# Attention with mixed heads: loads one per double step, half of them issued by GpSimd

## The chip, the cores and the metric

The kernel runs on one core of a Trainium2 chip. The metric is the time of one execution on the device in microseconds (us), lower is better; for the kernel before, three executions without a profile and one with it are shown.

## What is computed

Per batch (4 of them, 12 heads, 448 positions, 64 per head), scores of all heads are mixed by a 12 x 12 matrix before the softmax and by another one after it. The result goes through a token mixer and a channel mixer:

```python
scores = scale * np.matmul(q, k.transpose(0, 1, 3, 2))
scores = np.einsum('bhij,hg->bgij', scores, w_pre)
attn = softmax(scores)                      # over the last axis
attn = np.einsum('bhij,hg->bgij', attn, w_post)
x = np.matmul(attn, v)                      # then heads are joined: [4, 448, 768]
u = x + (np.maximum(x^T @ w_tok1, 0) @ w_tok2)^T
out = u + np.maximum(u @ w_ch1, 0) @ w_ch2
```

## The kernel before, in words

**Tiles.** A batch has four row tiles of 120, 120, 120 and 88 rows, so there are 16 tiles T. For a tile, `qk` (L140) computes the scores of a pair of heads in six calls and copies them to an SBUF tile `s`, on ScalarE (L156) or VectorE (L154). To mix heads on TensorE, the heads of ten rows have to lie along the partitions: `regroup` (L162, L164) moves them by a DMA from `s` into one of eight tiles `r`. There are 180 such groups.

**Steps.** Two groups make a step. `pre` (L166, L172) mixes the heads, `mx` (L180) takes the maximum on VectorE, `ex` (L189) the exponential on ScalarE, `rec` (L194) the reciprocal of the sums on VectorE and the product e with it on GpSimd (L203). `post` (L205, L214) mixes the heads again, `turn` (L229) transposes in blocks on VectorE, and `av` (L233, L246) multiplies by v for a pair of head pairs, ends in a copy on ScalarE (L253) and the sum x on GpSimd (L255), and leaves a store of x that `store` (L262) issues on SP later.

**Double steps.** The loop over J (L521) writes the program out, two steps at a time, and each engine runs its instructions in that order. Double step J holds the post of steps 2J and 2J+1, the softmax of the next two, the mixing of the two after those, the score groups that the table `score[J]` asks for and the value groups of `value[J]`. At its end come the four regroupings for steps 2J+8 and 2J+9 (L601) and the loads of `loads[J + 1]` (L604). A regrouping writes into an r that the mixing of the same double step has just read.

**Loads.** `load_q`, `load_k` and `load_v` (L104 to L135) fetch q of a tile, k of a batch in three pieces of two head pairs, and v of a batch in four parts. A load of q or k is two DMAs, one for partitions 0 to 63 and one for 64 to 127; the table `one` (L268) has SP issue both. Parts 2 and 3 of v are three DMAs each, which swap the halves of the partitions. Regroupings, loads and stores of x are all issued by SP and wait there in order. L505 to L514 fill the table of loads.

**Beginning and end.** Before the loop the first q and k are issued by SP and ScalarE, then q of tile 1 and part 0 of v by SP (L284, L285); the six score groups of tile 0 and the first eight regroupings follow (L310 to L313), and four score groups of tile 1 (L486). The last double steps and the stages after the loop (from L607) convert weights and run the two mixers; from about 330 us on they are long runs of matmuls.

Of the kernel before, what the change touches and what calls it, by code (L numbers as in the profile page):

```python
# [19 lines left out]
B, H, S, D = 4, 12, 448, 64  # L20
DM = H * D
DT, DC = 256, 1536
JT = 4
IT = [(0, 120), (120, 120), (240, 120), (360, 88)]
GR = 10
HP = H // 2
# [10 lines left out]
def attn_mixer_kernel(  # L37
# [12 lines left out]
    nc = tc.nc  # L50
# [34 lines left out]
    AT, V = {}, {}  # L85
# [15 lines left out]
    NT = len(first)  # L101
    first.append(NG)

    def load_k(b, h, m, eng):  # L104
        if b not in K:
            K[b] = early.tile([128, HP, S], F32, tag="k", bufs=2, name="k")
        for s in range(2):
            o = HP * s + h
            eng[s].dma_start(out=K[b][64 * s:64 * s + 64, h:h + m, :], in_=k[b, :, o:o + m, :])

    def load_q(T, h, m, eng):
        b, t = divmod(T, 4)
        i0, n = IT[t]
        if T not in Q:
            Q[T] = early.tile([128, HP, 120], F32, tag="q", bufs=3, name="q")
            if n < QP[t]:
                nc.gpsimd.memset(Q[T][:, :, n:QP[t]], 0.0)
        for s in range(2):
            o = H * i0 + (HP * s + h) * n
            eng[s].dma_start(  # L120
                out=Q[T][64 * s:64 * s + 64, h:h + m, :n],
                in_=q[b, :, o:o + m * n].rearrange("p (h i) -> p h i", h=m),
            )

    def load_v(b, part):
        if b not in V:
            V[b] = late.tile([128, H, JT, D], F32, tag="v", bufs=2, name="v")
        hs = slice(3 * part, 3 * part + 3)
        if part < 2:
            nc.sync.dma_start(out=V[b][:, hs], in_=v[b, :, hs])  # L130
            return
        lower, upper = slice(0, 64), slice(64, 128)
        nc.sync.dma_start(out=V[b][upper, hs, :3], in_=v[b, lower, hs, :3])
        nc.sync.dma_start(out=V[b][lower, hs, :3], in_=v[b, upper, hs, :3])
        nc.sync.dma_start(out=V[b][upper, hs, 3], in_=v[b, upper, hs, 3])  # L135

    def pair(tag, name):
        return (ps if tag == "pre" else ps_w).tile([128, 2, 512], F32, tag=tag, bufs=2, name=name)

    def qk(T, h, home="w", dve=False):  # L140
        b, t = divmod(T, 4)
        n = IT[t][1]
        if T not in S_t:
            S_t[T] = early.tile([120, H, S], F32, tag="s", name="s")
        p = pair(home, "qk")
        for c in (0, 64):
            m = min(64, QP[t] - c)
            for s in range(2):
                r = slice(64 * s, 64 * s + 64)
                nc.tensor.matmul(  # L150
                    out=p[c:c + m, s, :S], lhsT=Q[T][r, h, c:c + m], rhs=K[b][r, h, :], start=True, stop=True
                )
        if dve:
            nc.vector.tensor_copy(out=S_t[T][:n, h::HP, :], in_=p[:n, :, :S])  # L154
        else:
            nc.scalar.copy(out=S_t[T][:n, h::HP, :], in_=p[:n, :, :S])  # L156
# [109 lines left out]

    two = (nc.sync, nc.scalar)
    one = (nc.sync, nc.sync)  # L268
    load_q(0, 0, 2, two)
    load_k(0, 0, 1, two)  # L270
    load_k(0, 1, 2, two)
# [10 lines left out]
    for r in rt:  # L282
        nc.gpsimd.memset(r[:4], 0.0)
    load_q(1, 0, HP, one)  # L284
    load_v(0, 0)  # L285
    wz = et[0][:, 0].bitcast(BF16)
    nc.vector.memset(et[0], 0.0)
    for i in range(WARM):
# [4 lines left out]
    for x in range(2):  # L293
        ps_ = slice(64 * x, 64 * x + 64)
        nc.vector.tensor_tensor(
            out=kpre[ps_, :60].rearrange("p (i g) -> p i g", i=5),
# [5 lines left out]
    for s in range(2):  # L302
        ps_ = slice(64 * s, 64 * s + 64)
        for hf in range(2):
            nc.gpsimd.tensor_tensor(
                out=kpost[ps_, 32 * hf:32 * hf + 30].rearrange("p (g i) -> p g i", g=6),
# [165 lines left out]
    sf = [f // 2 for f in first]  # L472
    sl = [(f - 1) // 2 for f in first[1:]]
    loads = {J: [] for J in range(-2, ND)}
    score = {J: [] for J in range(-2, ND)}
    value = {J: [] for J in range(-2, ND)}
    for T in range(NT - 1):
        J = (sl[T] + 1) // 2
        n = sf[T + 2] // 2 - J
        if sf[T + 2] % 2 and sf[T + 2] // 2 > (sf[NT - 1] - 8) // 2:  # L480
            n += 1
        n = min(3, n)
        for hp in range(3):
            value[J + min(hp, n - 1)].append((T, hp))
    for h in range(HP):
        if h < 4:  # L486
            qk(1, h, ("pre", "w")[h % 2], h % 2 == 0)
        else:
            score[h - 6].append((1, h))
    for T in range(2, NT):  # L490
        hi = (sf[T] - 8) // 2
        lo = max((sl[T - 2] - 8) // 2 + 1 + (T == 4), hi - 2)
# [7 lines left out]
    uses = {}  # L500
    for J in range(-2, ND):
        score[J].sort()
        for T, h in score[J]:
            uses.setdefault((T, h), J)
    for T in range(2, NT):  # L505
        loads[max(-2, uses[T, 0] - 2)].append((load_q, T, 0, HP, one))
    for J, part in ((-1, 2), (0, 1), (2, 3)):
        loads[J].append((load_v, 0, part))
    for b in range(1, B):
        for h in range(0, HP, 2):  # L510
            J = uses[4 * b, 0] - 5 + h // 2
            loads[uses[4 * b, h] - 2 if b == 1 else J].append((load_k, b, h, 2, one))
        for part in range(JT):
            loads[sf[4 * b + 1] // 2 - 6 + part].append((load_v, b, part))  # L514

    def step(i):
        return steps[i] if 0 <= i < NS else []
# [284 lines left out]
```

## Time and profile before

| | |
|---|---|
| three runs without a profile | 748.48, 749.40, 750.58 us; median 749.4 |
| the profiled execution | 757.26 us, its span 755.50 us |
| TensorE clock granted | 1.00 of full speed |
| busy, share of the span | TensorE 97%, VectorE 54%, ScalarE 43%, GpSimd 40% |
| DMA on SP's queue (q1) | 66080 packets, 102.96 MB |
| DMA on GpSimd's queue (q0) | 96 packets, 0.03 MB |

The page shows one execution by the chip's own profiler. Busy times of TensorE are modelled, since its matmuls overlap; so its 97% says that gaps are few, not that it is at its peak. "issue" among the waits is idle time that ended with nothing that the profile shows. SP's rows are DMAs that it issues; their duration is the issuing, not the transfer. A post at L214 opens each double step, so the distance of two posts is the time of a double step.

### The profile page before, as it was taken

The numbers are of one execution on the slowest core, as the hardware profiler recorded it, in microseconds if no ns is written. First come the engines' busy times: TensorE is split into PE (matmuls) and PEld (weight loads), VectorE is DVE, ScalarE is ACT, GpSimd is POOL, SyncE is SP. The second block draws the span as 40 slices with busy tenths as digits, with TensorE's granted clock in tenths as the row PEclk, the third lists the DMA queues.
The fourth block names the chain that finished last, engine by engine and source line by source line (L and its number), as shares of the span: only waits on it lengthen the run. The fifth ranks groups of instructions, "written<-read, shape, count | busy, mean of one in ns | idle before, by whom it ended". The sixth has DMA issues, their size and how long they took to land. (4 is left out here: it accounts for less than half of the span.)

```text
span 755.5 us, 21850 instructions
## 1 busy us (share of the span) xinstructions
PE 735.6 (97%) x9209; PEld 570.5 (76%) x9209; DVE 410.7 (54%) x746; ACT 328.4 (43%) x732; POOL 303.7 (40%) x253
## 2 busy tenths in 40 slices
PE   8898999999999999899999999999999999999997
PEld 3354565556556555589988999999999999999997
DVE  3775676666766877778999999520004000220002
ACT  3776766776777777455544444300002000200000
POOL 3564665566656677757778777000000000000000
PEclk9999999999999999999999999999999999999999
DMA  6787667567756644735757655340003000020002
GB/s 180 240 232 213 199 194 229 190 192 217 231 175 228 217 165 159 265 104 198 252 178 221 169 170 162 147 146 1 1 1 146 1 1 1 0 74 1 0 1 74
DMA packets 66754, 105.27 MB, mean 139 GB/s; under 512 B 22835, under 2 KB 54624, under 8 KB 66144
## 3 DMA queue, kind: packets, MB, share of 16 engines
q1 hardware_dynamic: 66080, 102.96, 42.9%
q8 instruction: 73, 1.20, 0.7%
q10 hardware_dynamic: 480, 0.87, 0.5%
q14 instruction: 25, 0.20, 0.1%
q0 software_dynamic: 96, 0.03, 0.0%
HBM read 48.79 MB, written 16.52 MB: 86 GB/s over the span
## 5 line engine op out<-in xcount | busy, mean ns | idle before, releaser
L203 POOL TENSOR_TENSOR e<-e,sm 128x896 f32<-128x896 f32 x90 | 149.5, 1680 | 71.1 <-ACT e L189 25.9
L629 DVE SCALAR_TENSOR_TENSOR rl<-pc,rh 128x448 fp32r<-128x448 f32 x48 | 29.8, 621 | 218.7 <-ACT rh L628 218.7
L229 DVE STREAM_TRANSPOSE at<-post 128x896 f32<-128x896 f32 (+1 forms) x98 | 99.6, 1026 | 74.5 <-PE post L214 74.4
L628 ACT ACTIVATE rh<-pc 128x448 fp32r<-128x448 f32 x48 | 26.0, 542 | 232.9 <-PE pc L634 232.9
L189 ACT ACTIVATE e<-pre,sm 128x448 f32<-128x448 f32 x180 | 113.0, 640 | 5.5 <-DVE sm L198 4.8
L156 ACT COPY s<-qk 120x896 f32<-120x896 f32 (+1 forms) x91 | 81.6, 906 | 74.2 <-PE qk L150 70.5
L632 PE MATMUL pc<-u,w 128*128 128x448 f32 x288 | 105.3, 366 | 0.9 <-DVE u L665 0.9
L634 PE MATMUL pc<-u,w 128*128 128x448 f32 x288 | 105.2, 365 | 0.0
L633 PE MATMUL pc<-u,w 128*128 128x448 f32 x288 | 105.2, 365 | 0.0
L633 PE MATMUL po<-rl,w 128*128 128x448 f32 x288 | 105.2, 365 | 0.0
L634 PE MATMUL po<-rh,w 128*128 128x448 f32 x288 | 105.2, 365 | 0.0
L632 PE MATMUL po<-rh,w 128*128 128x448 f32 x288 | 105.2, 365 | 0.0
L180 DVE TENSOR_REDUCE sm<-pre 128x2 f32<-128x896 f32 x90 | 94.7, 1076 | 12.2 <-PE pre L172 12.1
L172 PE MATMUL pre<-r,kpre 64*64 64x448 f32 (+1 forms) x720 | 90.1, 550 | 4.0 <-DMA r<-s 2.7
L150 PE MATMUL qk<-k,q 64*64 64x448 f32 (+2 forms) x768 | 91.3, 542 | 2.7 <-issue 1.3
L246 PEld LDWEIGHTS av<-at,v 64*64 64x64 f32 x2688 | 73.8, 132 | 21.5 <-ACT s L156 10.4
L214 PE MATMUL post<-e,kpost 64*32 64x256 f32 (+1 forms) x2880 | 86.8, 355 | 3.1 <-issue 2.8
L422 POOL TENSOR_SCALAR cv_g<-cv_g 128x384 f32<-128x384 f32 (+1 forms) x52 | 82.3, 1585 | 18.2 <-ACT cv_g L416 18.2
L246 PE MATMUL av<-at,v 64*64 64x120 f32 (+1 forms) x2688 | 78.1, 259 | 3.0 <-issue 2.5
L214 PEld LDWEIGHTS post<-e,kpost 64*32 64x32 f32 x2880 | 51.0, 106 | 31.8 <-issue 21.5
L150 PEld LDWEIGHTS qk<-k,q 64*64 64x64 f32 (+2 forms) x768 | 28.8, 128 | 48.2 <-issue 20.5
L632 PEld LDWEIGHTS pc<-u,w 128*128 128x128 f32 x288 | 54.1, 188 | 5.5 <-DVE u L665 1.2
(78 smaller groups left out, 941.8 us busy)
## 6 DMA issues: line engine op xcount, KB each, us to landing
r<-s SPq DMA_DIRECT2D x172, 210.0 KB
cv_r<-in_w_ch_dram SPq DMA_DIRECT2D x48, 384.0 KB
xr<-x_dr SPq DMA_DIRECT2D x8, 672.0 KB
u_dr<-u SPq DMA_DIRECT2D x24, 224.0 KB
ur<-u_dr SPq DMA_DIRECT2D x4, 1344.0 KB
out_dram<-ur SPq DMA_DIRECT2D x24, 224.0 KB
k<-in_k_dram SPq DMA_DIRECT2D x20, 224.0 KB
x_dr<-x SPq DMA_DIRECT2D x36, 120.0 KB
```

Of the source, the lines that this page charges most:

```text
L150: nc.tensor.matmul(out=p[c:c + m, s, :S], lhsT=Q[T][r, h, c:c + m], rhs=K[b][r, h, :], start=True, stop=True)
L172: nc.tensor.matmul(out=p[64 * s:64 * s + 64, x, :S], lhsT=kpre[k], rhs=rt[a % NR][k], start=True, stop=True)
L180: nc.vector.tensor_reduce(out=s[:m, 0:2], in_=PP[st[0]][:m, :, :S], axis=AX.X, op=ALU.max, negate=True)
L189: nc.scalar.activation(out=E[st[0]][:m, x, :], in_=p[:m, x, :S], func=ACTF.Exp, bias=s[:m, x:x + 1], scale=1.0, accum_out=s[:m, 2 + 2 * x: ...
L203: nc.gpsimd.tensor_tensor(out=e[:m], in0=e[:m], in1=w.to_broadcast([m, 2, S]), op=ALU.mult)
L214: nc.tensor.matmul(out=p[32 * a:32 * a + 32, s, :S].rearrange("p (x f) -> p x f", x=2)[:, :, o:o + 32 * m], lhsT=kpost[k, 32 * hf:32 * hf ...
L229: nc.vector.transpose(out=AT[T][:, c:c + s1 - s0, :], in_=p[:, s0:s1, :S],)
L246: nc.tensor.matmul(out=p[64 * s:64 * s + 64, r, 10 * w * u:10 * w * (u + 1)], lhsT=V[b][k, 6 * u + h, j, :], rhs=at_[k, :w, :, f:f + 5], s ...
L422: nc.gpsimd.tensor_scalar(out=g[:P], in0=g[:P], scalar1=MAG_MIN, scalar2=MAG_MAX, op0=ALU.max, op1=ALU.min,)
L632: nc.tensor.matmul(out=p, lhsT=a[0], rhs=x[0], start=first, stop=False)
L633: nc.tensor.matmul(out=p, lhsT=a[0], rhs=x[1], start=False, stop=False)
L634: nc.tensor.matmul(out=p, lhsT=a[1], rhs=x[0], start=False, stop=last)
```

## The change

The loads get a table of their own so that, with two exceptions, a double step has one load; the first part of v comes in the loop, and q of tile 2 takes its place ahead of the loop. All six score groups of tile 1 are written ahead of the loop. The upper half of each q load from tile 3 on, and of each k load of batches 1 to 3, is issued on GpSimd's DMA queue; that makes 13 + 9 = 22 DMAs there. Parts 2 and 3 of v are two DMAs with all four blocks each.

```diff
--- before.py
+++ after.py
@@ -130,9 +130,8 @@
             nc.sync.dma_start(out=V[b][:, hs], in_=v[b, :, hs])
             return
         lower, upper = slice(0, 64), slice(64, 128)
-        nc.sync.dma_start(out=V[b][upper, hs, :3], in_=v[b, lower, hs, :3])
-        nc.sync.dma_start(out=V[b][lower, hs, :3], in_=v[b, upper, hs, :3])
-        nc.sync.dma_start(out=V[b][upper, hs, 3], in_=v[b, upper, hs, 3])
+        nc.sync.dma_start(out=V[b][upper, hs], in_=v[b, lower, hs])
+        nc.sync.dma_start(out=V[b][lower, hs], in_=v[b, upper, hs])
 
     def pair(tag, name):
         return (ps if tag == "pre" else ps_w).tile([128, 2, 512], F32, tag=tag, bufs=2, name=name)
@@ -266,6 +265,7 @@
 
     two = (nc.sync, nc.scalar)
     one = (nc.sync, nc.sync)
+    mixed = (nc.sync, nc.gpsimd)
     load_q(0, 0, 2, two)
     load_k(0, 0, 1, two)
     load_k(0, 1, 2, two)
@@ -282,7 +282,7 @@
     for r in rt:
         nc.gpsimd.memset(r[:4], 0.0)
     load_q(1, 0, HP, one)
-    load_v(0, 0)
+    load_q(2, 0, HP, one)
     wz = et[0][:, 0].bitcast(BF16)
     nc.vector.memset(et[0], 0.0)
     for i in range(WARM):
@@ -483,10 +483,7 @@
         for hp in range(3):
             value[J + min(hp, n - 1)].append((T, hp))
     for h in range(HP):
-        if h < 4:
-            qk(1, h, ("pre", "w")[h % 2], h % 2 == 0)
-        else:
-            score[h - 6].append((1, h))
+        qk(1, h, ("pre", "w")[h % 2], h % 2 == 0)
     for T in range(2, NT):
         hi = (sf[T] - 8) // 2
         lo = max((sl[T - 2] - 8) // 2 + 1 + (T == 4), hi - 2)
@@ -502,16 +499,28 @@
         score[J].sort()
         for T, h in score[J]:
             uses.setdefault((T, h), J)
-    for T in range(2, NT):
-        loads[max(-2, uses[T, 0] - 2)].append((load_q, T, 0, HP, one))
-    for J, part in ((-1, 2), (0, 1), (2, 3)):
-        loads[J].append((load_v, 0, part))
-    for b in range(1, B):
-        for h in range(0, HP, 2):
-            J = uses[4 * b, 0] - 5 + h // 2
-            loads[uses[4 * b, h] - 2 if b == 1 else J].append((load_k, b, h, 2, one))
-        for part in range(JT):
-            loads[sf[4 * b + 1] // 2 - 6 + part].append((load_v, b, part))
+    for T in range(3, NT):
+        loads[uses[T, 0] - 2].append((load_q, T, 0, HP, mixed))
+
+    def place(J, pieces):
+        for a in pieces:
+            while loads[J]:
+                J += 1
+            loads[J].append(a)
+
+    for b in range(B):
+        heads = [(load_k, b, h, 2, mixed) for h in range(0, HP, 2)]
+        parts = [(load_v, b, part) for part in (0, 2, 1, 3)]
+        if b == 0:
+            for J, a in zip((-1, 0, 1, 2), parts):
+                loads[J].append(a)
+        else:
+            if b == 1:
+                for J, a in zip((3, 4, 5), heads):
+                    loads[J].append(a)
+            else:
+                place(uses[4 * b, 0] - 4, heads)
+            place(sf[4 * b + 1] // 2 - 7, parts)
 
     def step(i):
         return steps[i] if 0 <= i < NS else []
```

On SP, the double steps from about 43 to 57 us, before (q and k of the loads, r the regroupings, x_dr a store of x):

```order
L164 DMA r_99<-s 120x1x448
L164 DMA r_100<-s 120x1x448
L120 DMA q<-in_q_dram 64x720 x2
L109 DMA k<-in_k_dram 64x896 x4
L265 DMA x_dr_59<-x 256x1x120
L164 DMA r_93<-s 120x1x448
L164 DMA r_94<-s 120x1x448
L164 DMA r_95<-s 120x1x448
L164 DMA r_96<-s 120x1x448
L109 DMA k<-in_k_dram 64x896 x2
```

and now (line numbers are one lower from L135 on):

```order
L163 DMA r_95<-s 120x1x448
L163 DMA r_96<-s 120x1x448
L109 DMA k<-in_k_dram 64x896
L163 DMA r_97<-s 120x1x448
L163 DMA r_98<-s 120x1x448
L163 DMA r_99<-s 120x1x448
L163 DMA r_100<-s 120x1x448
L120 DMA q<-in_q_dram 64x720
L109 DMA k<-in_k_dram 64x896
L264 DMA x_dr_59<-x 256x1x120
L163 DMA r_93<-s 120x1x448
```

Of the six loads in a row two are left; one k half stands a double step earlier, and the other halves are gone from this queue.

On GpSimd, the same stretch, before (e is the product behind the softmax, x the sum behind the value matmuls):

```order
L203 TENSOR_TENSOR e_89<-e_89,sm_103 128x896
L203 TENSOR_TENSOR e_90<-e_90,sm_104 128x896
L255 TENSOR_TENSOR x<-y 128x2x12x10
L203 TENSOR_TENSOR e_91<-e_91,sm_105 128x896
L203 TENSOR_TENSOR e_92<-e_92,sm_106 128x896
L255 TENSOR_TENSOR x<-y 128x2x12x10
```

and now:

```order
L202 TENSOR_TENSOR e_89<-e_89,sm_103 128x896
L202 TENSOR_TENSOR e_90<-e_90,sm_104 128x896
L254 TENSOR_TENSOR x<-y 128x2x12x10
L120 DMA q<-in_q_dram 64x720
L109 DMA k<-in_k_dram 64x896
L202 TENSOR_TENSOR e_91<-e_91,sm_105 128x896
L202 TENSOR_TENSOR e_92<-e_92,sm_106 128x896
L254 TENSOR_TENSOR x<-y 128x2x12x10
L109 DMA k<-in_k_dram 64x896
```

Two halves of k and one of q stand here, each behind an x and ahead of the next two e.

On TensorE, the last score groups of tile 1 and the first two mixing groups, before:

```order
L150 MATMUL qk<-k,q 64x448 x2
L150 MATMUL qk<-k,q 56x448 x2
L172 MATMUL pre<-r_93,kpre 64x448
L172 MATMUL pre<-r_94,kpre 64x448
L172 MATMUL pre<-r_93,kpre 64x448
L172 MATMUL pre<-r_94,kpre 64x448
L150 MATMUL qk<-k,q 64x448 x2
L150 MATMUL qk<-k,q 56x448 x2
L172 MATMUL pre<-r_95,kpre 64x448
L172 MATMUL pre<-r_96,kpre 64x448
L172 MATMUL pre<-r_95,kpre 64x448
L172 MATMUL pre<-r_96,kpre 64x448
```

and now:

```order
L149 MATMUL qk<-k,q 64x448 x2
L149 MATMUL qk<-k,q 56x448 x2
L149 MATMUL qk<-k,q 64x448 x2
L149 MATMUL qk<-k,q 56x448 x2
L149 MATMUL qk<-k,q 64x448 x2
L149 MATMUL qk<-k,q 56x448 x2
L171 MATMUL pre<-r_93,kpre 64x448
L171 MATMUL pre<-r_94,kpre 64x448
L171 MATMUL pre<-r_93,kpre 64x448
L171 MATMUL pre<-r_94,kpre 64x448
L171 MATMUL pre<-r_95,kpre 64x448
L171 MATMUL pre<-r_96,kpre 64x448
```

The score group (1,4) that stood between the first two mixing groups, and (1,5) that came later, are now ahead of both.

## Rows read from the trace of the kernel before

**Rows 1.** The page, parts 1 and 3: busy time, and the instruction queue q8 (packets, MB, share).
```profile
PE 735.6 (97%) x9209; PEld 570.5 (76%) x9209; DVE 410.7 (54%) x746; ACT 328.4 (43%) x732; POOL 303.7 (40%) x253
...
q8 instruction: 73, 1.20, 0.7%
```

**Rows 2.** TensorE's waits, 20 to 320 us: total us, times, longest.
```profile
PE post L214 <- issue: 2.8, 2, 1.8
...
PE pre L172 <- DMA r<-s: 2.0, 2, 1.8
```

**Rows 3.** Timeline, TensorE: start us, us, what [idle before <-what ended it].
```profile
61.48 1.88 PE L214 MATMUL post<-e,kpost 64*32 64x256 f32 x64
...
67.08 0.53 PE L150 MATMUL qk<-k,q 64*56 64x448 f32 x1 [1.32 <-issue]
...
70.52 1.81 PE L214 MATMUL post<-e,kpost 64*32 64x256 f32 x53
...
74.13 0.65 PE L214 MATMUL post<-e,kpost 64*32 64x192 f32 x11 [1.79 <-issue]
...
80.15 1.86 PE L214 MATMUL post<-e,kpost 64*32 64x256 f32 x64
...
119.84 1.96 PE L214 MATMUL post<-e,kpost 64*32 64x256 f32 x62
...
122.78 0.62 PE L214 MATMUL post<-e,kpost 64*32 64x256 f32 x2 [0.98 <-issue]
...
128.01 1.87 PE L214 MATMUL post<-e,kpost 64*32 64x256 f32 x64
...
134.51 0.80 PE L214 MATMUL post<-e,kpost 64*32 64x256 f32 x24
...
141.03 1.88 PE L214 MATMUL post<-e,kpost 64*32 64x256 f32 x64
...
148.30 1.88 PE L214 MATMUL post<-e,kpost 64*32 64x256 f32 x64
```

**Rows 4.** Windows between these gaps: busy us and (x instructions) of each engine.
```profile
67.05:74.10 7.05, 5.25 (x126) 3.76 (x126) 2.21 (x2) 4.85 (x11) 2.15 (x2) 1.00 0.76 220
...
74.10:122.75 48.65, 47.67 (x1137) 28.13 (x1136) 32.18 (x60) 34.76 (x79) 28.75 (x24) 1.00 0.66 204
```

**Rows 5.** Windows of 5 us; the last three columns are PEclk, DMA share, GB/s.
```profile
45.00:50.00 5.00, 5.00 (x142) 3.42 (x136) 3.26 (x6) 3.75 (x8) 3.88 (x3) 1.00 0.68 235
...
50.00:55.00 5.00, 5.00 (x108) 2.74 (x91) 4.16 (x8) 3.39 (x8) 3.33 (x3) 1.00 0.94 252
...
60.00:65.00 5.00, 5.00 (x140) 3.25 (x136) 3.11 (x6) 3.94 (x10) 1.70 (x2) 1.00 0.91 209
...
80.00:85.00 5.00, 5.00 (x106) 2.38 (x101) 3.55 (x8) 3.63 (x10) 2.87 (x3) 1.00 0.60 198
```

**Rows 6.** Timeline, SP's queue: the loads at 50 us.
```profile
49.98 1.17 SPq L120 DMA_DIRECT2D q<-in_q_dram  x2
...
51.21 2.70 SPq L109 DMA_DIRECT2D k<-in_k_dram  x4
```

**Rows 7.** GpSimd: by line (min/median/max ns) and timeline; VectorE from part 5.
```profile
L279 POOL DMA_DIRECT2D kcat<-in_wcat_dram x1: 755/755/755, 1.4 to 1.4; - x1
...
L281 POOL DMA_DIRECT2D kcat<-in_wcat_dram x2: 518/530/542, 2.1 to 2.6; - x2
...
DMA to landing us min/median/max: 3.9/4.4/4.9
...
L203 POOL TENSOR_TENSOR e<-e,sm x79: 1677/1680/1683, 34.2 to 298.2; 128x896 f32<-128x896 f32 x79
...
57.67 3.32 POOL L203 TENSOR_TENSOR e<-e,sm 128x896 f32<-128x896 f32 x2 [1.21 <-ACT e L189]
...
L180 DVE TENSOR_REDUCE sm<-pre 128x2 f32<-128x896 f32 x90 | 94.7, 1076 | 12.2 <-PE pre L172 12.1
```

**Rows 8.** Timeline, SP and TensorE at the start of the attention stage.
```profile
20.76 1.37 SPq L120 DMA_DIRECT2D q<-in_q_dram  x2
...
22.42 1.23 PE L172 MATMUL pre<-r,kpre 64*64 64x448 f32 x5 [1.80 <-DMA r<-s]
```

## Prediction

> **What bounds the kernel now.** I read the page first, then the waits of TensorE, then the timeline around its longest gaps, then the DMA share there, and last SP's and GpSimd's own rows.
>
> The page says that TensorE has 735.6 us of busy time in a span of 755.5 us [rows 1]. No engine has to become faster for this kernel to gain; TensorE's gaps have to go. So the reader should list the gaps and ask of each what ended it. In the attention stage two kinds stand out [rows 2]: "issue", which is time in which TensorE waited for nothing that the profile shows, and "DMA r<-s", a regrouped tile that was not there yet.
>
> The "issue" gaps are odd: they cut a run of equal matmuls in two. At 67.08 a single qk record stands after a gap of 1.32 us; at 74.13 the last 11 of 64 post records come after 1.79 us; at 122.78 the last 2 of 64 after 0.98 us [rows 3]. Nothing inside such a run waits for data. What the three have in common is their distance in the instruction stream. Between the first and the second lie 126 + 126 = 252 matmul and weight-load records, between the second and the third 1137 + 1136 = 2273, which is 9 x 252.6 [rows 4]. The page's queue q8 fetched instructions in 73 transfers of 1.20 MB, 16.4 KB each [rows 1], and 2 x 9209 records over 73 are again 252. So TensorE's program comes in blocks of 252 records and their semaphore instructions, and these gaps are blocks that came late.
>
> The Trainium skill (Runtime: NRT & Kernel Launch, Instruction fetch mechanics) describes blocks of 256 instructions that the sequencer fetches ahead over its own DMA queue, and calls the cost of a block's end mostly hidden. The trace agrees on the block and not on the cost: three block ends cost this stage gaps of 1.32, 1.79 and 0.98 us.
>
> When do they come late? In the 5 us before 50 us the DMA engines were busy for 0.68 of the time; from 50 to 55 for 0.94 and from 60 to 65 for 0.91 [rows 5]. What came in between is on SP's queue: two q loads and four k loads in a row, 1.17 + 2.70 us of issuing, ahead of the next regroupings [rows 6]. The late blocks at 67 and 74 stand behind that burst.
>
> What the gaps cost is more than their length, since the engines behind TensorE run dry as well. Measured from one post to the next, the double steps from 61.48 and 70.52 took 9.04 and 9.63 us; the one from 141.03, with the same three score and one value matmul groups, took 7.27. That is 1.77 + 2.36 = 4.13 us. The one from 119.84 took 8.17 and its neighbour of the same make 6.50: 1.67 us [rows 3]. Together **5.8 us**.
>
> **The change, part by part.**
>
> *The score groups (1,4) and (1,5) and the q load of tile 2 go ahead of the first regroupings; the first v load goes behind.* On TensorE two score groups of about 1 us each move in front of the first mixing matmuls. Before, these waited for r anyway (a gap of 1.80 us at 22.42 [rows 8]) and the score groups stood between them. The r tiles are released by the same copies and go out on the same queue, so I expect the wait to stay, with TensorE idle a little longer in it and busy less later: 0 us. Bounds: the gain of that gap, 1.8 us, and a loss of one score group, 1 us. I take 0, since in either order it is r that the third mixing group waits for. The q load that is taken out behind regrouping 7 frees 1.37 us on SP [rows 8]; the next four regroupings start that much earlier, but after 20 us TensorE waited for r only twice, 2.0 us in all [rows 2], most of it in the gap already named.
>
> *One load per double step.* The burst of six DMAs at 50 us loses its first k pair to the double step before, where SP had none; the pair of a q and a k at 110 us is parted, likewise q with v later. Bytes stay the same, so the gain is only in how deep the queues get. Both ends: nothing (the blocks come late somewhere else) and the whole 5.8 us. I take three quarters, 4.4 us: one k group of the three at 50 us still stands with a q, and the step is one load smaller, not empty.
>
> *Upper halves on GpSimd's queue.* 22 DMAs leave SP, at about 0.6 us each (1.17 us for two q [rows 6]): that is 13 us over 250 us on a queue for which nobody waits: 0 us. On GpSimd they cost issue time. The only rows are the three small loads at the start: 0.53 us for 60 rows, 0.755 us for 120 [rows 7], so some 0.55 us for the 64 rows of a half; by the slope of 3.75 ns a row the four narrow q halves with 64 x 6 runs would take 0.55 + 320 x 0.00375 = 1.75 us. They stand behind the x sum of a double step, ahead of the next two products e. There GpSimd is idle for 1.21 us before e [rows 7], and the second e, done at 57.67 + 3.32 = 60.99, is used in the second half of the post that starts at 61.48 and takes 1.88 [rows 3], so at 62.4: 1.4 us more. The cover is 2.6 us; 0.55 and 1.75 lie inside it: 0 us. The other end would be the whole time to landing, 4.4 us [rows 7], which includes the transfer; I leave it to the tail. Queued behind the issue is e, and post waits for e. The loads themselves are asked for two double steps ahead, so a slower landing is no wait.
>
> The Trainium skill (SBUF — State Buffer, section SBUF: two separate sides) warns that GpSimd cannot write DMA descriptors while VectorE holds the port pair they share. Here the 79 products e took 1677 to 1683 ns beside a VectorE that is busy for 54% of the span [rows 1, 7], so no lockout shows for them; no row shows it for descriptors. By that rule each issue would grow by a VectorE instruction such as the maximum of 1.08 us [rows 7], to 1.65 us, still inside the cover.
>
> *v in two DMAs instead of three.* SP saves 8 issues of some 0.6 us, and runs of 768 B become 3 KB. Off the path: 0 us.
>
> Against these I set 0.2 us for small new waits. **Sum: 4.4 - 0.2 = 4.2 us.** The profiled execution took 757.26 us (span 755.50), 7.9 us above the median of 749.4 of the runs without a profile; which part of the program that extra belongs to cannot be read here, so I take the same 4.2 us off the median: **745.2 us**.
>
> **The rivals.**
>
> 1. *The stalls only move, or belong to the profiled execution.* The DMA engines move the same bytes in the same 300 us, at 0.6 to 0.9 busy in the stretches read [rows 5]; a late block may simply be another one. And the profiled run is longer than the others by more than all three stalls. For it speaks that excess; against it that the blocks between 80 and 120 us all came in time, mostly at one load per double step. Then the time is 749.4, at most 1 us off.
>
> 2. *Even loading never lets the queues drain: slower.* Now six double steps between 40 and 230 us have no load at all; after the change every one up to 250 us has one. If blocks then come late more often than three times, it is a loss: each costs about 5.8 / 3 = 1.9 us. Three late blocks is the point where it turns; at five the time is 749.4 + 3.9 = 753.3 us. For it speaks the DMA share of 0.9 that the burst reached; against it 0.60 at 80 us, in a double step that had one load [rows 5].
>
> 3. *GpSimd's issue is much dearer than 0.55 us.* Above the cover of 2.6 us each of the 22 pushes post; at 3.0 us that is 22 x 0.4 = 8.8 us against a gain of 4.2: 754.0 us. Against it speak the only rows there are.
>
> 4. *The Trainium skill's "mostly hidden" holds, and the "issue" gaps are something else* that loads do not touch. That is a rule of its own; worked out from rows it gives 749.4, since the burst would then cost nothing that shows. The counts of 252 and the place of two gaps behind the burst speak against it.
>
> **How the numbers follow.** A measurement of this kernel can tell about 0.3% (2.2 us) from no change, so "faster" means below 747.2 and "slower" above 751.6. The forecast (half of the 5.8 us or more comes back) has 0.57. Rival 1 has 0.25, rival 4 has 0.03, rival 2 has 0.11, rival 3 has 0.04. The range starts at 742.0: the whole 5.8 us and most of one r gap (1.6 us). It ends at 751.3, in the first part of rival 2: one late block more than now (749.4 + 1.9). What lies above is left out, about one in eight. The forecast's own range is 742 to 747.
>
> **What would show it.** Right: the double steps at about 61 and 70 us take 7.3 to 8 us, TensorE's "issue" waits between 20 and 310 us fall from 1.32 + 1.79 + 0.98 = 4.1 us to about 1, the DMA share around 60 us stays under 0.85, and GpSimd's issues take under 1 us with e's duration unchanged. Wrong: the same number of "issue" gaps at other multiples of 252 records; "POOL e" as what ends gaps before post; or a new wait of qk for k or q. The end stage from 330 us should be the same but earlier; if it absorbs the gain, then TensorE was not what it waited for.

## The result, and the profile after

The changed kernel takes 756.1 us (median of four runs, 754.8 to 758.0) against 749.9 us (median of four, 748.5 to 750.6) of the kernel before: a ratio of 1.0071, 95% interval 1.0049 to 1.0093, about 6 us **slower**. The forecast was 4.2 us faster, and its range ended at 751.3. Ratios in this document leave out the few runs that lie more than 1.5% above the fastest of their kernel.

What the page of the profiled execution (756.2 us) says of the whole, parts 1 and 3:

```profile
PE 734.7 (97%) x9209; PEld 571.1 (76%) x9209; DVE 412.7 (55%) x747; ACT 327.1 (43%) x731; POOL 315.5 (42%) x275
...
q1 hardware_dynamic: 59328, 99.09, 41.1%
q0 software_dynamic: 1152, 4.30, 2.5%
```

The work of TensorE is the same [rows 1]; 22 DMAs with 4.3 MB went to GpSimd's queue, as the change says. So what is lost has to be idle time. The shown profile of before can't tell where, since it took 757.26 us itself; a second one, below, can. TensorE's waits from 20 to 320 us, which answer to [rows 2]:

```profile
PE pre L171 <- DMA r<-s: 2.2, 3, 0.9
...
PE post L213 <- issue: 1.2, 2, 0.7
```

"issue" ahead of post fell from 2.8 to 1.2 us, as the forecast wanted. The timeline (columns as in [rows 3]), from the first post to the last, shows that the places did change as planned, too:

```profile
23.92 0.99 PE L213 MATMUL post<-e,kpost 64*32 64x256 f32 x32
...
34.56 1.81 PE L213 MATMUL post<-e,kpost 64*32 64x256 f32 x64
37.77 0.60 PE L171 MATMUL pre<-r,kpre 64*64 64x448 f32 x3 [0.52 <-DMA r<-s]
40.94 1.75 PE L213 MATMUL post<-e,kpost 64*32 64x256 f32 x64
45.07 0.60 PE L171 MATMUL pre<-r,kpre 64*64 64x448 f32 x3 [0.82 <-DMA r<-s]
48.11 0.60 PE L171 MATMUL pre<-r,kpre 64*64 64x448 f32 x3 [0.90 <-DMA r<-s]
51.28 1.82 PE L213 MATMUL post<-e,kpost 64*32 64x256 f32 x64
...
64.54 1.87 PE L213 MATMUL post<-e,kpost 64*32 64x256 f32 x64
71.81 1.88 PE L213 MATMUL post<-e,kpost 64*32 64x256 f32 x64
...
125.33 1.50 PE L213 MATMUL post<-e,kpost 64*32 64x256 f32 x36
127.30 0.98 PE L213 MATMUL post<-e,kpost 64*32 64x256 f32 x28 [0.46 <-issue]
132.89 0.64 PE L213 MATMUL post<-e,kpost 64*32 64x256 f32 x11
134.25 1.71 PE L213 MATMUL post<-e,kpost 64*32 64x192 f32 x53 [0.72 <-issue]
140.62 1.68 PE L213 MATMUL post<-e,kpost 64*32 64x256 f32 x56
...
320.88 0.99 PE L213 MATMUL post<-e,kpost 64*32 64x256 f32 x32
```

The double step from 64.54 takes 7.27 us, the time without a late block. But the one from 34.56 takes 6.38 and the one from 40.94 takes 10.34 us, with three waits for a regrouped tile r in them. What they should take stands in the first experiment below.

### The profile page after: what moved, and what is told of

Read it like the earlier page. It is cut to its first block, busy times and chain, and to the rows that moved or that the text cites. A ratio compares the mean times of both kernels' runs of the same rounds, so it can differ in the third digit from the quotient of the medians.

```text
span 754.4 us, 21884 instructions
## 1 busy us (share of the span) xinstructions
PE 734.7 (97%) x9209; PEld 571.1 (76%) x9209; DVE 412.7 (55%) x747; ACT 327.1 (43%) x731; POOL 315.5 (42%) x275
## 5 line engine op out<-in xcount | busy, mean ns | idle before, releaser
L171 PE MATMUL pre<-r,kpre 64*64 64x448 f32 (+1 forms) x720 | 92.2, 550 | 5.6 <-DMA r<-s 2.2
L213 PE MATMUL post<-e,kpost 64*32 64x192 f32 (+1 forms) x2880 | 86.1, 355 | 3.2 <-DVE sm L197 1.7
L171 PEld LDWEIGHTS pre<-r,kpre 64*64 64x64 f32 (+1 forms) x720 | 24.6, 132 | 45.2 <-issue 32.0
```

Of the source, the lines that this page charges most:

```text
L171: nc.tensor.matmul(out=p[64 * s:64 * s + 64, x, :S], lhsT=kpre[k], rhs=rt[a % NR][k], start=True, stop=True)
L213: nc.tensor.matmul(out=p[32 * a:32 * a + 32, s, :S].rearrange("p (x f) -> p x f", x=2)[:, :, o:o + 32 * m], lhsT=kpost[k, 32 * hf:32 * hf ...
```

## The experiments

Ratios are against the kernel before on the same chip, with 95% intervals. An experiment starts from the kernel before and makes one edit, where nothing else is said.

### Was there anything to win?

**The kernel before, profiled a second time** (no edit).

> The kernel before, unchanged, for a second profile. Theory A (the shown profile, 757.3 us against runs of 748.5 to 750.6, caught an execution with late instruction blocks that most executions do not have): about 750 us in the profile too, the double steps that took 9.04 and 9.63 us now take about 7.3, and hardly any 'issue' gap of over 0.5 us between 50 and 130 us. Theory B (the gaps are always there and the profile itself costs the rest): the same gaps at 67, 74 and 122 us.

0.9982 [0.9933, 1.0031], and the profile has none of the three late blocks:

```profile
24.55 2.12 PE L214 MATMUL post<-e,kpost 64*32 64x256 f32 x64
...
36.27 1.81 PE L214 MATMUL post<-e,kpost 64*32 64x256 f32 x64
41.58 1.81 PE L214 MATMUL post<-e,kpost 64*32 64x256 f32 x64
48.02 1.82 PE L214 MATMUL post<-e,kpost 64*32 64x256 f32 x64
54.46 1.83 PE L214 MATMUL post<-e,kpost 64*32 64x256 f32 x64
60.96 1.87 PE L214 MATMUL post<-e,kpost 64*32 64x256 f32 x64
68.21 1.88 PE L214 MATMUL post<-e,kpost 64*32 64x256 f32 x64
...
121.73 1.87 PE L214 MATMUL post<-e,kpost 64*32 64x256 f32 x64
128.23 1.86 PE L214 MATMUL post<-e,kpost 64*32 64x256 f32 x64
...
313.95 0.99 PE L214 MATMUL post<-e,kpost 64*32 64x256 f32 x32
```

The double step from 60.96 takes 7.25 us where the shown profile had 9.04 [rows 3], and the one from 121.73 takes 6.50 where it had 8.17. So the stalls of 5.8 us, on which the whole forecast stood, are not in every execution. Nor are they in most, by an estimate from the profiles: 24.55 us up to the first post, 289.4 from there to the last post (313.95), 433.0 behind it (755.5 - 322.46 in the shown profile) and 1.9 by which the time exceeds the span make 749 us, close to the medians of 749.4 to 751.8 us that the runs of this kernel have. This second profile took 755.92 us because its end stage, the two mixers behind the last post, was a slow one, which the last section shows.

This row set is also the right one to hold the changed kernel against: 6.38 against 5.31 and 10.34 against 6.44 are 5.0 us lost before 52 us, of which the first double step, earlier and shorter, gives a part back (the post of 64.54 comes 3.6 us behind that of 60.96); the double steps from 125.33 and 132.89 (7.56 and 7.73 against some 6.5) lose 2.3 more. From the first post to the last the changed kernel takes 297.0 us against 289.4, and 433.5 us are left behind the last post: the loss lies in the attention stage.

**How much could lighter loading win at most?** Two kernels leave loads out: 19 upper halves, then all 44 later halves of q and k. The loads of v stay in both.

```diff
-        for s in range(2):
+        for s in range(2 if b < 2 else 1):
...
-        for s in range(2):
+        for s in range(2 if T < 3 else 1):
```
```diff
+        if b:
+            K[b] = K[0]
+            return
...
+        if T > 2:
+            Q[T] = Q[T % 3]
+            return
```

> The kernel before without 19 of its later half loads (the upper halves of q from tile 3 on and of k of batches 2 and 3: the tiles keep what an earlier tile put there). It shows how much a lighter attention stage can win at all. Theory A (in an ordinary execution the loads cost the kernel before almost nothing, so there was nothing to win): 0.996 to 1.001. Theory B (loads that delay regroupings and instruction blocks cost it several us in every execution, as the forecast had it): 0.990 to 0.995.

> The kernel before without any of the 44 later half loads of q and k (all tiles read q of tiles 0 to 2 and k of batch 0). Theory A: 0.995 to 1.000. Theory B: 0.985 to 0.993, with the attention stage some 5 us or more shorter than the 284 us (from the first post at L214 to the last double step's) of the second profile of before.

0.9984 [0.9966, 1.0002] and 0.9969 [0.9948, 0.9991]. Without a single one of these loads the kernel is 2.3 us faster (at most 3.9): the ceiling for any better way to issue the loads of q and k lies below the 4.2 us of the forecast. From the first post to the last the second profile of before takes 313.95 - 24.55 = 289.4 us, this one 315.69 - 27.33 = 288.4:

```profile
27.33 1.84 PE L220 MATMUL post<-e,kpost 64*32 64x256 f32 x64
...
315.69 0.99 PE L220 MATMUL post<-e,kpost 64*32 64x256 f32 x32
```

### Which part loses?

**The changed kernel without one of its parts:** all halves back on SP, then the beginning of before.

```diff
-    mixed = (nc.sync, nc.gpsimd)
+    mixed = (nc.sync, nc.sync)
```
```diff
-    load_q(2, 0, HP, one)
+    load_v(0, 0)
...
-            for J, a in zip((-1, 0, 1, 2), parts):
-                loads[J].append(a)
+            for J, part in ((-1, 2), (0, 1), (2, 3)):
+                loads[J].append((load_v, 0, part))
```

> The changed kernel with all later halves of q and k on SP's queue again; the new table of loads and the new beginning stay. Crowding theory (six loads in the short double steps between 25 and 50 us fill the DMA queues, and regrouped tiles r land late): still about 756 us, TensorE still waits for r between 35 and 50 us. Queue theory (loads on a second queue cut in between the regroupings at the DMA engines): back to about 750 us, no wait for r there.

> The changed kernel with the beginning of the kernel before: part 0 of v ahead of the regroupings, q of tile 2 behind regrouping 7, score groups (1,4) and (1,5) in the loop, the other parts of v of batch 0 at the old places; the table from batch 1 on, GpSimd's queue and v in two DMAs stay. Crowding theory: one load less between 25 and 50 us, so most of the 6 us come back, 750 to 752 us. Queue theory: 755 to 757 us.

Without GpSimd's queue 1.0049 [1.0004, 1.0093], with the old beginning 1.0021 [0.9984, 1.0058]. Both point below the 1.0071 of the whole change, though the intervals overlap with its own; the first, just clear of 1, says that a loss is left without GpSimd's queue.

**One part alone**, on the kernel before: the upper halves on GpSimd; the new beginning (twice); v in two DMAs; the new table for k and v of batches 1 to 3.

```diff
+    mixed = (nc.sync, nc.gpsimd)
...
-        loads[max(-2, uses[T, 0] - 2)].append((load_q, T, 0, HP, one))
+        loads[max(-2, uses[T, 0] - 2)].append((load_q, T, 0, HP, one if T == 2 else mixed))
...
-            loads[uses[4 * b, h] - 2 if b == 1 else J].append((load_k, b, h, 2, one))
+            loads[uses[4 * b, h] - 2 if b == 1 else J].append((load_k, b, h, 2, mixed))
```
```diff
-    load_v(0, 0)
+    load_q(2, 0, HP, one)
...
-        if h < 4:
...
+        qk(1, h, ("pre", "w")[h % 2], h % 2 == 0)
...
-    for J, part in ((-1, 2), (0, 1), (2, 3)):
+    for J, part in ((-1, 0), (0, 2), (1, 1), (2, 3)):
```
```diff
-        nc.sync.dma_start(out=V[b][upper, hs, :3], in_=v[b, lower, hs, :3])
...
+        nc.sync.dma_start(out=V[b][upper, hs], in_=v[b, lower, hs])
+        nc.sync.dma_start(out=V[b][lower, hs], in_=v[b, upper, hs])
```
```diff
+            for J, a in zip((3, 4, 5), heads):
+                loads[J].append(a)
...
+            place(uses[4 * b, 0] - 4, heads)
+        place(sf[4 * b + 1] // 2 - 7, parts)
```

> The kernel before with the upper halves of q from tile 3 on and of later k on GpSimd's queue; table, beginning and v as before. Crowding theory: 749 to 751 us. Queue theory: 755 to 757 us, with waits for r in the double steps after a load.

> The kernel before with the new beginning alone: q of tile 2 ahead of the regroupings, part 0 of v behind them, score groups (1,4) and (1,5) ahead of the loop, v of batch 0 in the order 0, 2, 1, 3 at double steps -1 to 2. Everything on SP, v in three DMAs, table from batch 1 on as before. If the beginning crowds the early double steps: 752 to 755 us. If it does not: 748 to 750 us, the first post at about 24 us or earlier.

> The kernel before with the new beginning alone, a second time: the first time gave 1.0031 [0.9997, 1.0066] and its profiled execution was a disturbed one, so its profile could not be read. Theory A (part 0 of v now lands in the short double steps, so that regroupings of tile 2 and 3 come late): 1.002 to 1.005, and double steps between 30 and 48 us that take 2 us or more longer than the 6.4 us of before. Theory B (the beginning costs nothing): 0.998 to 1.001, and these double steps as before.

> The kernel before with parts 2 and 3 of v in two DMAs of all four blocks instead of three. Crowding theory: these move 144 + 48 KB more evenly and a little more in all (192 x 2 against 144 x 2 + 48 KB), so 749 to 751 us. If the two larger DMAs hold up the regroupings behind them: 752 to 754 us with waits for r after each.

> The kernel before with the new table alone for k and v of batches 1 to 3 (one load per double step), all on SP, beginning and v in three DMAs as before. If even spreading is good by itself: 747 to 749 us and no late block around 60 to 75 us. If the k piece that is moved into the double step that had no load is what crowds: 752 to 754 us with a long double step at 40 us.

| part alone | ratio | interval |
|---|---|---|
| upper halves on GpSimd | 1.0060 | 1.0014 to 1.0107 |
| new beginning | 1.0031, then 1.0019 | 0.9997 to 1.0066, 0.9994 to 1.0043 |
| v in two DMAs | 1.0012 | 0.9988 to 1.0037 |
| new table | 0.9988 | 0.9957 to 1.0020 |

Only GpSimd's queue is clear by itself, and its size is uncertain: five of the ten runs took 751.2 to 754.0 us and five 758.3 to 762.3. The end stage has two speeds, which lie 7 us apart in the profiles (last section); which one a run without a profile had isn't known. The median of the lower five is 752.0 us, 0.3% above that of before's runs below 757 us (749.7).

In the profile of this kernel (753.98 us) TensorE waits for no r between 20 and 320 us. What stands there instead are runs of equal matmuls cut by "issue", the kind of gap that the forecast read as a late instruction block:

```profile
61.42 1.34 PE L246 MATMUL av<-at,v 64*64 64x120 f32 x38 [1.82 <-issue]
68.09 0.53 PE L150 MATMUL qk<-k,q 64*56 64x448 f32 x1 [1.11 <-issue]
```

The double steps around them, from 53.97 and 62.69, take 8.72 and 8.83 us instead of 6.50 and 7.25.

The double step from about 41 us, where the changed kernel loses most, is not lengthened by these halves alone. It takes 6.44 us before, 6.49 with the new table, 6.54 with the halves on GpSimd, 7.65 with the new beginning and 8.54 with v in two DMAs; 8.42 in the changed kernel with all on SP, 10.34 in the whole. These are single profiles, and a kernel below that has the loads of before (the one with memsets) takes 7.32 there, so about 1 us may be chance. How the parts add up is not shown.

**The changed kernel on another chip.**

> The changed kernel a second time, on this chip. Theory A (the loss is in every execution, early, where TensorE waits for r, and in a few places later that change from one execution to the next): 1.004 to 1.009, with double steps between 30 and 50 us that take 3 to 5 us longer in sum than before. Theory B (the first ratio of 1.0071 was of one chip): 0.999 to 1.003.

1.0101 [1.0064, 1.0137]. The loss sits in the same places:

```profile
34.71 1.81 PE L213 MATMUL post<-e,kpost 64*32 64x256 f32 x64
40.52 1.74 PE L213 MATMUL post<-e,kpost 64*32 64x256 f32 x64
43.02 0.93 PE L171 MATMUL pre<-r,kpre 64*64 64x448 f32 x2 [0.75 <-DMA r<-s]
44.44 0.60 PE L171 MATMUL pre<-r,kpre 64*64 64x448 f32 x3 [0.49 <-DMA r<-s]
49.69 1.82 PE L213 MATMUL post<-e,kpost 64*32 64x256 f32 x64
56.29 1.80 PE L213 MATMUL post<-e,kpost 64*32 64x256 f32 x64
60.35 1.64 PE L171 MATMUL pre<-r,kpre 64*64 64x448 f32 x5 [0.59 <-DMA r<-s]
64.57 1.68 PE L213 MATMUL post<-e,kpost 64*32 64x256 f32 x56
```

5.81, 9.17 and 8.28 us against 5.31, 6.44 and 6.50: again 5 us before 65 us. From the first post to the last it takes 296.9 us (24.08 to 321.01), as in the first profile of the changed kernel.

**Why r is late there** is argued and not shown, since the profile has no landing times for regroupings. A window of 5 us (the last two columns are the DMA share and GB/s), first of the second profile of before, then of the changed kernel:

```profile
40.00:45.00 5.00, 5.00 (x100) 2.26 (x104) 4.30 (x7) 4.09 (x10) 3.00 (x3) 1.00 0.81 240
```
```profile
40.00:45.00 5.00, 3.62 (x76) 1.54 (x69) 3.54 (x7) 3.75 (x10) 2.43 (x3) 1.00 0.90 200
```

In this window the DMA engines are busier and move less: 200 GB/s at a share of 0.90, against 240 at 0.81. And the lateness goes round: a score tile s (there are two) is free again only when its regroupings have read it, so ScalarE waits too, and then the next regroupings start late. ScalarE in the changed kernel:

```profile
48.39 0.90 ACT L155 COPY s<-qk 88x896 f32<-88x896 f32 x1 [4.64 <-DMA r<-s]
```

### What is it about a DMA on GpSimd's queue?

Three things could cost: GpSimd's time to issue, the transfer, or its place. First the dose (both halves on GpSimd, 44 DMAs), then the same 22 halves issued ahead of the sum x instead of behind it (upper_loads issues those of loads[J + 1]).

```diff
+    mixed = (nc.gpsimd, nc.gpsimd)
...
```
```diff
             if eb:
                 rec(eb)
+            upper_loads(J + 1)
...
             for a in vs:
                 av(*a)
```

> The kernel before, with both halves of the 22 later q and k loads issued on GpSimd's DMA queue: the dose of the upper halves alone doubled (44 DMAs). The upper halves alone gave a ratio of 1.006 [1.0014, 1.0107]. Theory A (transfers on a second queue run beside the regroupings and make them, or an instruction block, late): about twice that, 1.008 to 1.014, and longer waits of TensorE for r. Theory B (what costs is GpSimd's time to issue them, ahead of the products e): about the same as A in the time, 1.008 to 1.014, but with e starting late and post waiting for GpSimd. Theory C (1.006 was chance; of its ten runs five happened to be above 758 us): 0.998 to 1.003.

> The kernel before with the 22 upper halves on GpSimd, but issued ahead of the sum x of the double step, where GpSimd waits for ScalarE's copy anyway, instead of behind it and ahead of the next two products e (there they gave 1.006 [1.0014, 1.0107]). Theory A1 (the cost is GpSimd's time): 0.998 to 1.002. Theory A2 (the cost is the DMA itself and its transfer): 1.003 to 1.009.

44 DMAs gave 1.0094 [1.0065, 1.0122]. The earlier place, where the issue itself stands in an idle time, gave not less but more: 1.0130 [1.0102, 1.0158]. In both kernels the fastest run (755.3 and 758.6 us) is slower than every run of before beside it, and both profiles have the fast end stage, so these two losses don't hang on its speed. At the earlier place the halves are issued beside the four regroupings of the same double step (a k half at 114.33 us, the regroupings from 112.94 to 116.57). Two of its long double steps, the ones from 48.31 (9.68 us) and from 120.90 (9.99 us), have these gaps:

```profile
56.98 1.08 PE L246 MATMUL av<-at,v 64*64 64x120 f32 x12 [2.44 <-issue]
...
128.10 2.86 PE L246 MATMUL av<-at,v 64*64 64x120 f32 x56 [2.06 <-ACT s L156]
```

The first is a run cut by "issue"; the second waits for ScalarE's copy into a score tile s, which itself had waited 3.55 us for a DMA (by the profile a store of x). The halves themselves land hardly later than behind x (median of k 7.2 us against 6.7).

In the kernel with 44 DMAs, too, the time goes to "issue", where the forecast had looked for it:

```profile
PE post L214 <- issue: 3.9, 3, 1.5
...
PE pre L172 <- issue: 2.4, 2, 1.9
```

So the three profiles of kernels that differ from before only by halves on GpSimd's queue have two, four and two "issue" gaps of 1.1 us or more between 20 and 310 us. Of the eleven profiles with all DMAs of the attention stage on SP, only the shown one of before has any (two). In the five others that have DMAs on GpSimd's queue, the two of the changed kernel among them, none is longer than 1.02 us. So it is suggested, and not shown, that such halves make instruction blocks late.

Then GpSimd's time and the DMA apart: 22 times three memsets of 0.17 us, without a DMA; 22 DMAs of 1 KB into a tile that nobody reads, on GpSimd; the same 22 on SP; 44 of them on GpSimd.

```diff
...
+        for _ in range(3):
+            nc.gpsimd.memset(junk, 0.0)
```
```diff
...
+        nc.gpsimd.dma_start(out=junk[:, j:j + 4], in_=q[0, :, j:j + 4])
```

> The kernel before with, in place of the 22 tiny DMAs, three memsets each on GpSimd (about 3 x 0.18 = 0.54 us, the time that the issue of one DMA takes there), into a tile that nobody reads. Theory A1 (the cost is GpSimd's time, ahead of the products e): 1.003 to 1.006. Theory A2 (the cost is the DMA that GpSimd issues, not its time): 0.998 to 1.002.

> The kernel before, all its loads on SP as they were, and 22 additional DMAs of 1 KB (64 rows of 16 bytes into a tile that nobody reads) issued by GpSimd at the places where the upper halves stood: GpSimd's issue time without the transfers. They are an addition, 22 KB in all. Theory A (the transfers beside the regroupings): 0.998 to 1.002. Theory B (the issue time on GpSimd): 1.004 to 1.008, as the upper halves gave. Theory C (nothing of it is real): 0.998 to 1.002, as A.

> The kernel before with the same 22 tiny DMAs of 1 KB at the same places, issued by SP instead of GpSimd (they are an addition). On GpSimd they gave 1.0047 [1.0024, 1.0071]. Theory A (a DMA issued by GpSimd has a cost of its own): 0.998 to 1.002. Theory B (any 22 more DMAs, or the tile that moves the others in memory, cost that): 1.003 to 1.006.

> The kernel before with 44 tiny DMAs on GpSimd, two at each of the 22 places. Theory A (each DMA of GpSimd has a cost): about twice 1.0047, so 1.007 to 1.011. Theory C (1.0047 is what any small change of this kernel's program may give, whatever it is, since the kernel of before lies at the low end of many neighbours): 1.001 to 1.006, without a dose.

| added to before | ratio | interval |
|---|---|---|
| 0.5 us of GpSimd's time, 22 times | 0.9986 | 0.9961 to 1.0012 |
| 22 tiny DMAs on GpSimd | 1.0047 | 1.0024 to 1.0071 |
| 22 tiny DMAs on SP | 1.0066 | 1.0037 to 1.0095 |
| 44 tiny DMAs on GpSimd | 1.0054 | 1.0034 to 1.0074 |

GpSimd's time costs nothing. A DMA costs on either queue, even with no bytes worth counting, so theory B of the tiny DMAs on SP holds against the one that blames GpSimd alone; its other half, the tile that moves the others in memory, falls with the memsets, which have a tile of the same size per partition. On SP one mechanism can be read: three issues of 0.6 us stand among the loads from 52 us on, ahead of the next regroupings, and TensorE waits for r:

```profile
53.54 0.59 SPq L515 DMA_DIRECT2D junk<-in_q_dram  x1
54.17 2.02 SPq L110 DMA_DIRECT2D k<-in_k_dram  x2
56.24 0.60 SPq L515 DMA_DIRECT2D junk<-in_q_dram  x1
56.88 1.24 SPq L110 DMA_DIRECT2D k<-in_k_dram  x2
58.16 0.59 SPq L515 DMA_DIRECT2D junk<-in_q_dram  x1
...
59.56 3.83 SPq L165 DMA_DIRECT2D r<-s  x4
```
```profile
63.72 1.35 PE L173 MATMUL pre<-r,kpre 64*64 64x448 f32 x5 [1.26 <-DMA r<-s]
```

That double step takes 9.32 us instead of 7.25. On GpSimd this way is not there, and 44 tiny DMAs cost no more than 22: 1.0054 lies below theory A's range and inside theory C's (any small change, without a dose), against which the memsets speak, a small change that cost nothing. Why the tiny DMAs cost anything on GpSimd stays **open**, and with it how much of the 1.006 is the bytes and how much merely one more DMA: the intervals lie over each other.

### A version that might beat both

The new table with SP alone, and the two halves of each load parted by two regroupings, so that no load stands in one piece ahead of four of them.

```diff
-        for fn, *a in loads.get(J + 1, ()):
-            fn(*a)
+            for fn, *a in loads.get(J + 1, ()):
+                if fn is not load_v:
+                    fn(*a, (0,) if st is sts[0] else (1,))
...
```

> A version that might beat both: the beginning of before, the new table for k and v of batches 1 to 3, all on SP (this alone gave 0.9988 [0.9957, 1.0020]), and the two halves of each q and k load parted, one behind the first two regroupings of a double step and one behind the other two. Theory A (regroupings come late because loads stand in one piece ahead of them): 0.994 to 0.998. Theory B (the queues are as full whatever the order of SP): 0.998 to 1.002.

1.0030 [1.0014, 1.0046]: slower. No version that was run beats the kernel before by more than its uncertainty while it does the whole work; the new table alone is the nearest.

## Why the prediction was wrong

**The step that failed first** is the sum "together 5.8 us" and "I take three quarters, 4.4 us". It read three late blocks in one profiled execution and took them for the kernel's. A second execution has none, and by the estimate above most have none. The text even had the warning in hand: the profiled execution lay 7.9 us above the median, outside all three runs, and it wrote that "which part of the program that extra belongs to cannot be read here" and took the gain off the median all the same. Rival 1 in its second half ("or belong to the profiled execution") was right on this. Late blocks do exist, and the kernel with 44 DMAs on GpSimd has more of them; only an ordinary execution of the kernel before has none to take away, and all 44 later half loads of q and k together are worth 2.3 us.

**The step that gave the sign** is "upper halves on GpSimd's queue: 0 us". Its price was right (0.55 us forecast for a full half, medians of 557 and 555 ns measured), e stayed at 1.68 us [rows 7], and the cover was right, since 0.5 us of GpSimd's time cost nothing. The narrow q halves, for which the slope gave 1.75 us, took no more than 0.72, and so no issue grew to the 1.65 us that were worked out for the shared port. Rival 3 falls with that. What failed is the sentence behind it: "a slower landing is no wait". It asked who waits for the load and not what else comes late beside it. The term measured 0.6% (4.5 us, interval 1 to 8; some 0.3% if the upper five runs had the slow end stage) instead of 0, and 44 halves or an earlier place measured 0.9% and 1.3%. In the profile of these halves alone the time goes to "issue" gaps, in the changed kernel to waits for r. That both come from transfers which share the DMA engines with the loads is argued, and why even a tiny DMA costs is open. The Trainium skill (DMA: Bandwidth & Descriptors, section Issuing engines are not separate DMA queues) says that DMAs run on the same 16 engines and interleave whichever engine starts them, so that a second issuer saves only issue time. The measurement agrees that nothing else was saved, and goes further: here it was a loss. No run shows the interleaving itself.

**New beginning: 0 us.** Measured +0.3% and +0.2% (2.3 and 1.4 us), neither clear of zero; both lie outside the bounds (gain 1.8, loss 1), and their intervals reach into them. The first post did not come earlier by it: it stands at 23.92 in the changed kernel, at 24.61 with the new beginning alone, and between 23.65 (with memsets) and 26.33 (the shown profile) in kernels that begin like the one before. A v load now lands in the short double steps, and in the second profile the double step from 41 us takes 1.2 us more.

**One load per double step, 4.4 us.** Measured 0.9 us (loss of 1.5 to gain of 3.2): the sign may be right, the size is not. **v in two DMAs, 0 us.** Measured +0.9 us with an interval across zero.

The four measured terms, -0.9 + 4.5 + 1.9 + 0.9 (the beginning as the mean of its two), make 6.4 us, about what the whole measured (5.3 and 7.6 by its two ratios); each of them is uncertain by 2 us or more, so the agreement shows little.

**Rival 2** had the sign and half of the mechanism: the DMA share does rise (0.90 for 0.81 from 40 to 45 us). But it counted late blocks, and in the changed kernel there are two small ones before 310 us (0.46 and 0.72 us); most of the loss is on r and s before 52 us, for which no rival had a price. Late blocks did come more often in the profiles of kernels with nothing but halves on GpSimd, whose loads are not spread more evenly. Of the signs named beforehand, the double steps at 61 and 70 us (7.27 us), the fall of "issue" and e's duration came out as forecast, and the share around 60 us just missed (0.87 for 0.85). The first two did not tell a gain from an ordinary execution of the kernel before, which has the same 7.25 us and hardly an "issue" gap; a sign has to be checked against that first.

## What to carry to other kernels

A stall in one profiled execution is a candidate, not a price: profile the unchanged kernel a second time, above all when the profiled run lies outside the timed ones, before a gain is booked. Before loads are spread or moved, take them out altogether once; that gives the ceiling of everything that could be done to them. And a DMA that nobody waits for can still cost more than its issue time: measure it alone, in its place, before it is booked at nothing.

## What the runs showed of the hardware that was not expected

The two mixer stages run at two speeds, 2% apart, at the same granted clock of 1.00. Windows of 100 us that are almost all matmuls, in the shown profile of before, in its second one, and in the second of the changed kernel:

```profile
540.00:640.00 100.00, 100.00 (x495) 92.72 (x494) 15.46 (x26) 10.42 (x20) 0.00 (x0) 1.00 0.08 28
```
```profile
540.00:640.00 100.00, 100.00 (x486) 90.83 (x485) 15.61 (x26) 10.42 (x20) 0.00 (x0) 1.00 0.08 28
```
```profile
540.00:640.00 100.00, 100.00 (x485) 90.83 (x484) 15.61 (x26) 10.43 (x20) 0.00 (x0) 1.00 0.08 28
```

495 matmuls against 486 and 485, and not by kernel: of the two profiles of before one is fast and one slow, and so of the two of the changed kernel. Behind the last post the fast ones take 433.0 and 433.5 us, the slow ones 440.1 and 440.4. That is 7 us of the time between two executions, about as much as the change itself, and it explains why the second profile of before took 755.9 us with an attention stage of 289.4 us where the shown one has 296.1. What sets it was not found.
